# One-hop corner transfers, a later tile stage and one direct pair fewer in a spectral and gated-MLP kernel

## The chip, the cores and the metric

The kernel runs on one core of a Trainium2 chip. The metric is the device time in microseconds (us) of one execution.

## The reference

For x of 2048 tokens by 576 features (all float32), a two-dimensional Fourier filter and a gated MLP are mixed by a gate of each token:

```python
g = sigmoid((x * gate_w).sum(-1, keepdims=True))
X = jnp.fft.rfft2(x, axes=(-2, -1)) * (w_r + 1j * w_i)
a = jnp.fft.irfft2(X, s=(2048, 576), axes=(-2, -1))
h = jax.nn.gelu(x @ w_gate, approximate=True) * (x @ w_up)   # 576 -> 4608
b = h @ w_down                                               # 4608 -> 576
out = g * a + (1 - g) * b
```

## The kernel before

**The MLP, on TensorE.** Each float32 operand is kept as a high and a low part, and a product is three matmuls: high by high, high by low, low by high. The 4608 hidden features are 36 blocks of 128, taken two at a time ("a pair"), and the tokens are two halves of 1024; half by half that makes 36 pair turns, in the order of the string `PLAN` (line 35). A letter "c" is a direct pair (`conv`): eight chains of 14 matmuls of 512 columns, that is 112. An "s" is a pair by block products (`products`): the operands are cut into 2 by 2 blocks, and seven products of sums stand for eight; with two chains of seven matmuls each that is 98. Both kinds end in the same eight `down` turns (one for 128 tokens, 12 matmuls of 288 columns into PSUM tile `pdn`, two buffers), which ScalarE empties into `stg` (four buffers, L978); POOL adds them to the DRAM tiles `yd` by accumulating DMA (L965). `PLAN` is 2 direct pairs, 10 as block products, 10 direct, 14 as block products. The direct ones are needed where the operand sums of the block products have no room: `operands` puts those sums in tile `sx`, which lies in the same memory as `til`, the spectral tiles.

Weights are loaded by SP into `wq` (L834 direct, L1145 block products, L839 for `down`), split by ScalarE (`copy`, L218) and VectorE (L856, L1160, L1177).

**The filter, beside it.** `spectral` is a Python generator that emits the transforms a few instructions at a time. Row transforms (along the 576 features) run on VectorE and ScalarE in tile `rows`; column transforms (along the 2048 tokens) are a 4 by 4 tile stage (butterflies L96 to L104, twiddles L116 to L132) over the 16 blocks of `til`, and, in `columns`, a matrix product of length 128 of each block on TensorE (L283), the filter weights, and the product back. Then comes the inverse tile stage (`last_tiles`), half by half of the blocks, stores to the DRAM tile `bw` (`kept`, L733), and in the last stretch of block products `fetch` (L644), `fetched_rows` and `inverse_rows`, whose result is added to `yd`.

**How the order is made.** Each engine runs its instructions in the order in which they are emitted. `gap` is called after every product chain and every `down` turn: it runs what was put off to this gap, and lets the generator emit as long as its credit lasts. Credit is what the matmuls emitted since then take on PE; each VectorE instruction emitted is charged. A bare `yield None` ends the generator's turn in this gap. A direct pair has 24 gaps, a block-product pair 22. When the second stretch of "s" begins, `operands(1)` has to be done, and at the last pair the generator has to be empty; otherwise `gap` is called without matmuls.

**The column stage.** `columns` takes the 16 blocks in turn, six steps (gaps) each; `kb` is the block. A block's two halves, real and imaginary, lie so that the transform needs one quarter of each exchanged between partitions 0 to 63 and 64 to 127: the corners. `corner` does this in two hops over a small buffer `cns` (in `hx`), two transfers of 64 partitions out (L272, L273) and two back (L269, L270), all issued by SP, once ahead of the forward product and once behind the inverse one:

```python
if g == 0: v = product(0, kb, xh, xl); load_ww(kb + 1); corner(kb + 2, 0, False)
if g == 1: copy(xh2, two(Z[kb + 1])); corner(kb - 2, 2, True)
if g == 3: swap(); corner(kb + 2, 0, True); low(xl2, two(Z[kb + 1]), xh2)
if g == 4: w = product(1, kb - 1, yh, yl)      # copied back into Z[kb - 1]
if g == 5: filter_end(); corner(kb - 1, 2, False)
```

Beside this, `beside` emits the inverse butterfly of four blocks (`four`) five steps into the sixth block of each group, `while gone[0] < (4 * d + 5) * STEP + 5`.

## Time and profile before

| what | value |
|---|---|
| median of 3 runs | 1359.33 us (1356.89 to 1361.45) |
| profiled execution, its own time | 1353.73 us |
| its span, first to last instruction | 1352.0 us |
| granted TensorE clock, mean | 0.998 |
| DMA | 231.95 MB, mean 172 GB/s |
| direct pairs 12 to 21, with the column stage | about 425 to 847 us of the span |
| last stretch of block products | from about 847 us |

A page of the profile gives the busy time of each engine (PE is the matmuls, PEld the weight loads, DVE VectorE, ACT ScalarE, POOL GpSimd, SP the queue of the loads and stores), and the chain of work that ended last, which says what set the end. The views by window give the busy time in a stretch; the timeline shows in brackets how long an engine stood still ahead of an instruction and what released it. A matmul of 512 columns starts 0.23 us after the one before, though a row gives it 0.39.

### The profile page before, as it was taken

How to read it: one execution, taken by the hardware profiler on the slowest of the kernel's cores; microseconds unless marked ns; L12 is line 12 of the kernel's file. 1: busy time of each engine (PE TensorE's matmuls, PEld its weight loads, DVE VectorE, ACT ScalarE, POOL GpSimd, SP SyncE). 2: the span in 40 equal slices, each digit the busy share in tenths (PEclk: the TensorE clock that was granted, in tenths of full speed). 3: DMA queues.
4: the chain of work that ended last, by engine and by line, in shares of the span. 5: the costliest groups of instructions: out<-in, count | busy, mean ns of one | idle time of the engine just before them, and what ended most of it. 6: DMA issues, size and time to landing. Idle time of an engine off the chain costs nothing.

```text
span 1352.0 us, 20022 instructions
## 1 busy us (share of the span) xinstructions
PE 1335.8 (99%) x7353; PEld 1180.6 (87%) x7353; DVE 1112.5 (82%) x1566; ACT 839.3 (62%) x1446; POOL 263.3 (19%) x323
## 2 busy tenths in 40 slices
PE   9999999999999999999999999999999999999998
PEld 7888888888888888888888888888888888888887
DVE  7689999899898779777775885899996699998554
ACT  5766666666765445656654448666766766766762
POOL 0011212221212221222220111112222321122321
PEclk9999999999999999999999999999999999999999
DMA  8667776786667977999994776867668967766986
GB/s 313 200 144 152 149 140 138 180 196 127 120 115 148 226 169 171 208 234 257 253 226 136 218 207 139 214 127 133 129 133 152 219 130 134 134 130 130 166 189 176
DMA packets 112067, 231.95 MB, mean 172 GB/s; under 512 B 13024, under 2 KB 28896, under 8 KB 111584
## 3 DMA queue, kind: packets, MB, share of 16 engines
q0 software_dynamic: 44928, 90.98, 44.7%
q1 hardware_dynamic: 67040, 139.69, 31.4%
q8 instruction: 57, 0.93, 0.3%
q14 instruction: 42, 0.34, 0.1%
HBM read 124.09 MB, written 99.39 MB: 165 GB/s over the span
## 4 chain that ended last, share of the span: by engine, by line
PE 91%; ACT 2%; DVE 2%; DMA 2%; issue 1%; SPq 0%; DVEq 0%; ACTq 0%
PE pdn L952 32%; PE pgu L1195 6%; PE pgu L1197 6%; PE pgu L1196 6%; PE pone L1195 6%; PE pone L1197 5%; PE pone L1196 5%; PE pgu L877 4%; PE pgu L879 4%; PE pgu L878 4%; PE pgu L1198 3%; PE pone L1198 3%; PE pone L877 2%; PE pone L879 2%; PE pone L878 2%; PE pone L283 1%
## 5 line engine op out<-in xcount | busy, mean ns | idle before, releaser
L965 POOL DMA_DIRECT2D yd<-stg x264 | 229.0, 867 | 1011.4 <-ACT stg L978 789.5
L978 ACT ACTIVATE stg<-pdn,omg 128x576 f32<-128x576 f32 x276 | 204.2, 740 | 274.6 <-PE pdn L952 272.4
L952 PE MATMUL pdn<-dn,hb 128*128 128x288 f32 x2472 | 361.2, 295 | 0.3 <-DVE wq L1019 0.2
L952 PEld LDWEIGHTS pdn<-dn,hb 128*128 128x128 f32 x2472 | 347.7, 188 | 13.4 <-ACT stg L978 0.7
L218 ACT ACTIVATE gu<-wq 64x256 fp32r<-64x256 f32 (+4 forms) x365 | 236.1, 661 | 75.7 <-DVE gu L1160 54.3
L1160 DVE TENSOR_TENSOR gu<-wq,gu 128x768 fp32r<-128x768 f32 x168 | 159.7, 952 | 33.4 <-ACT gu L218 33.0
L952 PE MATMUL pdn<-dn,hx 128*128 128x288 f32 x960 | 148.3, 295 | 0.0
L952 PEld LDWEIGHTS pdn<-dn,hx 128*128 128x128 f32 x960 | 137.4, 188 | 4.1
L877 PE MATMUL pgu<-xhi,gu 128*128 128x512 f32 x276 | 108.7, 394 | 2.2 <-DVE gl L934 2.2
L878 PE MATMUL pgu<-xhi,gu 128*128 128x512 f32 x276 | 108.3, 392 | 0.0
L879 PE MATMUL pgu<-xlo,gu 128*128 128x512 f32 x276 | 108.2, 392 | 0.0
L1177 DVE TENSOR_TENSOR wq<-wq 128x768 f32<-128x768 f32 x96 | 91.2, 952 | 10.7 <-ACT gu L218 10.2
L218 ACT ACTIVATE hb<-gl 128x512 fp32r<-128x512 f32 x65 | 40.8, 628 | 50.0 <-DVE gl L934 47.8
L856 DVE TENSOR_TENSOR dn<-wq,dn 128x576 fp32r<-128x576 f32 x72 | 54.1, 752 | 10.8 <-ACT dn L218 10.7
L877 PEld LDWEIGHTS pgu<-xhi,gu 128*128 128x128 f32 x276 | 52.2, 189 | 11.6 <-DVE gl L934 3.0
L879 PEld LDWEIGHTS pgu<-xlo,gu 128*128 128x128 f32 x276 | 52.1, 189 | 11.6
L878 PEld LDWEIGHTS pgu<-xhi,gu 128*128 128x128 f32 x276 | 52.1, 189 | 8.5
L1195 PE MATMUL pgu<-xhi,gu 128*128 128x512 f32 x144 | 56.8, 394 | 2.7 <-ACT pgu L218 2.7
L1195 PE MATMUL pone<-xhi,gu 128*128 128x512 f32 x144 | 56.6, 393 | 0.1
L1195 PE MATMUL pgu<-sx,gu 128*128 128x512 f32 x144 | 56.5, 392 | 0.0
L1195 PE MATMUL pone<-sx,gu 128*128 128x512 f32 x144 | 56.4, 392 | 0.0
L1197 PE MATMUL pgu<-xlo,gu 128*128 128x512 f32 x144 | 56.2, 391 | 0.0
(246 smaller groups left out, 2829.7 us busy)
## 6 DMA issues: line engine op xcount, KB each, us to landing
yd<-stg POOLq DMA_DIRECT2D x264, 288.0 KB, 4.9
wq<-ws SPq DMA_DIRECT2D x96, 384.0 KB, 4.4
wq<-wd SPq DMA_DIRECT2D x72, 288.0 KB, 5.2
wq<-wgu SPq DMA_DIRECT2D x22, 640.0 KB, 6.3
colm<-col POOLq DMA_DIRECT2D x32, 256.0 KB, 6.3
misc<-wf SPq DMA_DIRECT2D x16, 290.0 KB, 6.0
hx<-til SPq DMA_DIRECT2D x64, 72.5 KB, 5.5
til<-hx SPq DMA_DIRECT2D x64, 72.5 KB, 4.4
```

The source lines that it names most:

```text
L218: act.activation(o, i, AF.Copy)
L877: pe.matmul(ps, w[:, 0, k, c], xhi[tb][:, k], start=k == 0, stop=False)
L878: pe.matmul(ps, w[:, 1, k, c], xhi[tb][:, k], start=False, stop=False)
L879: pe.matmul(ps, w[:, 0, k, c], xlo[tb][:, k], start=False, stop=False)
L952: pe.matmul(ps[half], h[:, l, c], d[:, k, half * HD:(half + 1) * HD], start=part == 0 and n == 0, stop=part == 1 and n == 2)
L965: pl.dma_start(yd[u], o, accum_op=ALU.add)
L978: put(u, lambda o: act.activation(o.rearrange("p (c k) -> p c k", c=2), v[:, :, 0:HD], AF.Copy, scale=omg[:, u:u + 1]), i == 0)
L1160: vec.tensor_tensor(o, x.rearrange("p (c k) -> p c k", c=3), f(w[:, 256:1024]).rearrange("p (c k) -> p c k", c=3), ALU.subtract)
L1177: at(lead, lambda: vec.tensor_tensor(o, u, v, ALU.subtract))
L1195: pe.matmul(ps, hi, xh[:, t], start=start and t == 0, stop=False, skip_group_check=True)
L1196: pe.matmul(ps, lo, xh[:, t], start=False, stop=False, skip_group_check=True)
L1197: pe.matmul(ps, hi, xl[:, t], start=False, stop=False, skip_group_check=True)
```

## The change

Three things change together:

- `PLAN` has 9 direct pairs in the middle instead of 10, and 15 pairs as block products at the end instead of 14.
- A corner exchange is one hop of four transfers of 64 partitions instead of two hops of two. Ahead of the forward product the whole block, exchanged, goes from `til` into one of two buffers `near` (in `hx`); behind the inverse product the result is first copied into one of two buffers `far` (in `xraw`), and goes from there, exchanged, into `til`. The inverse butterflies may start two steps earlier, and the loop is one block shorter.
- The inverse tile stage of half one (blocks e = 0 and 1 of each group) leaves the direct stretch. `keep` stores the four-block results to `bw` within the column stage, two stores of 290 KB each time; in the last stretch `late_tiles(0)` and `late_tiles(1)` load four blocks into `tmp` (1160 KB), do twiddles and butterfly there, and write `rows` directly. `last_tiles(1)`, `kept(1)` and `operands(1)` follow the columns as before.

```diff
-PLAN = "c" * 2 + "s" * 10 + "c" * 10 + "s" * 14
+PLAN = "c" * 2 + "s" * 10 + "c" * 9 + "s" * 15
...
+            near = [f(hx)[:, SW * i:SW * (i + 1)] for i in range(2)]
+            far = [flat[:, SW * i:SW * (i + 1)] for i in range(1, 3)]
-            def corner(kb, slot, back):
+            def corner(kb, back):
...
-                z, c = two(Z[kb]), cns[:, slot + kb % 2]
+                o, i = two(near[kb % 2]), two(Z[kb])
                 if back:
-                    nc.sync.dma_start(z[0:64, 1], c[0:64])
-                    nc.sync.dma_start(z[64:128, 0], c[64:128])
-                else:
-                    nc.sync.dma_start(c[0:64], z[64:128, 0])
-                    nc.sync.dma_start(c[64:128], z[0:64, 1])
+                    o, i = i, two(far[kb % 2])
+                for c in range(2):
+                    for al in range(2):
+                        nc.sync.dma_start(o[64 * c:64 * c + 64, al], i[64 * al:64 * al + 64, c])
...
-                    while gone[0] < (4 * d + 5) * STEP + 5:
+                    while gone[0] < (4 * d + 5) * STEP + 3:
                         yield None
                     yield from four(d, range(4), sp, 1)
+                    keep(d)
+                    yield None
...
-            for kb in range(18):
+            for kb in range(17):
...
-                            corner(kb + 2, 0, False)
+                            corner(kb + 2, False)
...
-                            copy(xh2, two(Z[kb + 1]))
-                        corner(kb - 2, 2, True)
+                            copy(xh, near[(kb + 1) % 2])
...
-                            corner(kb + 2, 0, True)
                         if kb + 1 < 16:
-                            low(xl2, two(Z[kb + 1]), xh2)
+                            low(xl, near[(kb + 1) % 2], xh)
...
-                                copy(two(Z[kb - 1])[:, al], w[al][:, :NK])
+                                copy(two(far[(kb - 1) % 2])[:, al], w[al][:, :NK])
...
-                            corner(kb - 1, 2, False)
+                            corner(kb - 1, True)
...
+        def keep(d):
+            for e in range(2):
+                c = slice(SW * (4 * e + d), SW * (4 * e + d + 1))
+                nc.sync.dma_start(bw[:, c], til[0][:, c])
+
+        def late_tiles(e):
+
+            nc.sync.dma_start(tmp[:, 0:4 * SW], bw[:, 4 * SW * e:4 * SW * (e + 1)])
+            for _ in range(5):
+                yield None
...
+            x = [tmp[:, SW * i:SW * (i + 1)] for i in range(4)]
+            *tmps, sp = (rows[:, i:i + SW] for i in (UNIT, UNIT + SW, 3 * UNIT, 3 * UNIT + SW))
...
+            if o:
+                yield from _twiddles(vec, act, lambda d, e: x[d], lambda d, e: x[d][:, re], lambda d, e: x[d][:, im],
+                                     [((k, e), o * k) for k in range(1, 4)], tmps, 1, 0.39)
+            yield from _butterfly(vec, lambda i: x[i], lambda i: x[i][:, re], lambda i: x[i][:, im],
+                                  range(4), sp, 1, (0.69, 0.39))
...
+                pl.memset(rows.rearrange("p (c g k) -> p c g k", c=2, g=4)[:, :, g, 2 * KF:], 0.0)
...
             yield from last_tiles(1)
-            yield from with_stores(last_tiles(0), kept(1))
-            yield from with_stores(operands(1), kept(0))
+            yield from with_stores(operands(1), kept(1))
             yield from until(3)
-            fetch(0, 0, places_of[0])
-            yield from fetched_rows(0)
+            yield from late_tiles(0)
+            yield from late_tiles(1)
+            fetch(1, 0, places_of[1])
             yield from inverse_rows(0)
-            yield from fetched_rows(1)
+            yield from fetched_rows()
             yield from inverse_rows(1)
```

Three places show how this moves instructions. The first is SP's queue in the middle of the column stage: `hx` and `til` are the corners, `wf` the filter's weights. Before, one block's turn:

```order
L261 DMA tmp<-wf 128x580 x2
L272 DMA hx<-til 64x290
L273 DMA hx<-til 64x290
L269 DMA til<-hx 64x290
L270 DMA til<-hx 64x290
L269 DMA til<-hx 64x290
L270 DMA til<-hx 64x290
L272 DMA hx<-til 64x290
L273 DMA hx<-til 64x290
```

Now, a turn at which a group of four blocks has been finished, and the next one:

```order
L260 DMA tmp<-wf 128x580 x2
L274 DMA hx<-til 64x290 x4
L640 DMA bw<-til 128x580 x2
L274 DMA til<-xraw 64x290 x4
L260 DMA misc<-wf 128x580 x2
L274 DMA hx<-til 64x290 x4
L860 DMA wq<-wgu 128x1280
L274 DMA til<-xraw 64x290 x4
```

A turn still has eight corner transfers, but none that needs another one of its block to have landed; the stores of `keep` stand between them.

The second is SP's queue where the direct pairs end and the last stretch begins (`ws` and `wd` are weights, `xhi`, `xlo`, `misc` and `tmp` the places for `bw`). Before:

```order
L733 DMA bw<-til 128x1160 x4
L839 DMA wq<-wd 128x576 x2
L733 DMA bw<-til 128x1160 x4
L1145 DMA wq<-ws 128x768 x4
L839 DMA wq<-wd 128x576 x2
L644 DMA xhi_64<-bw 128x2x290
L644 DMA xlo_66<-bw 128x2x290
L644 DMA misc<-bw 128x2x290 x2
L644 DMA tmp<-bw 128x2x290 x4
```

Now:

```order
L759 DMA bw<-til 128x1160 x4
L1171 DMA wq<-ws 128x768 x4
L865 DMA wq<-wd 128x576 x2
L644 DMA tmp<-bw 128x2320
L1171 DMA wq<-ws 128x768 x4
L865 DMA wq<-wd 128x576 x2
L644 DMA tmp<-bw 128x2320
L1171 DMA wq<-ws 128x768 x4
L865 DMA wq<-wd 128x576 x2
L675 DMA xhi_64<-bw 128x2x290
```

Four of the eight wide stores are gone, and two loads of four blocks stand a pair apart among the weights where eight loads stood together.

The third is VectorE at the end of pair 11, the last block-product pair ahead of the direct ones; the instruction on `gu` makes the low part of a direct pair's weights, the one on `xraw` and `pgu` is the last gelu product of pair 11. Before:

```order
L1233 TENSOR_TENSOR xraw<-xraw,pone 128x512
L856 TENSOR_TENSOR gu_71<-wq,gu_71 128x1280
L1219 TENSOR_TENSOR hx<-xraw,hx 128x512
L96 TENSOR_TENSOR rows<-rows 128x40x32
L1216 TENSOR_TENSOR xraw<-xraw 128x512
L101 TENSOR_TENSOR rows<-rows 128x20x32
L1290 TENSOR_TENSOR xraw<-xraw,pgu 128x512
L101 TENSOR_TENSOR rows<-rows 128x20x32 x3
```

Now:

```order
L1259 TENSOR_TENSOR xraw<-xraw,pone 128x512
L1245 TENSOR_TENSOR hx<-xraw,hx 128x512
L1242 TENSOR_TENSOR xraw<-xraw 128x512
L101 TENSOR_TENSOR rows<-rows 128x20x32
L1316 TENSOR_TENSOR xraw<-xraw,pgu 128x512
L882 TENSOR_TENSOR gu_72<-wq,gu_72 128x1280
L101 TENSOR_TENSOR rows<-rows 128x20x32 x2
```

With nine direct pairs the first one's weights go into buffer `gu_72` instead of `gu_71`, which comes free later, and their low part moves from ahead of that product to behind it.

More of the change, by code (lines that the diff above doesn't have):

```diff
@@ L653, in fetched_rows @@
             s2 = sgn[:, None, :].to_broadcast([P, 2, KF])
[L654 to L655 removed]
+            for b in range(2):
+                for i, x in enumerate(places_of[1]):
                     g, c = divmod(i, 2)
```

53 lines of the change are left out of this document (28 added, 25 removed).

## The prediction

> **What bounds the kernel now.** I read the page first (busy times and the chain), then the stages by window, then the PE waits inside the stages that lose time. The page's busy row and the chain:
>
> ```profile
> PE 1335.8 (99%) x7353; PEld 1180.6 (87%) x7353; DVE 1112.5 (82%) x1566; ACT 839.3 (62%) x1446; POOL 263.3 (19%) x323
> PE 91%; ACT 2%; DVE 2%; DMA 2%; issue 1%; SPq 0%; DVEq 0%; ACTq 0%
> ```
>
> TensorE is the bound: 91% of the chain. So time can go in two ways only: fewer matmuls, or fewer holes between them. The stages (columns: stretch, its length, busy us and instructions of PE, PEld, DVE, ACT, POOL, granted clock, DMA share, GB/s) show where the holes are:
>
> ```profile
> 535.00:720.00 185.00, 179.67 (x1007) 159.60 (x1006) 141.03 (x228) 109.73 (x187) 42.59 (x58) 0.99 0.92 228
> 720.00:860.00 140.00, 139.77 (x759) 122.59 (x758) 96.83 (x135) 79.74 (x130) 17.21 (x20) 1.00 0.69 182
> 860.00:1232.00 372.00, 372.00 (x2054) 329.34 (x2053) 338.91 (x447) 250.75 (x443) 80.41 (x94) 1.00 0.73 142
> 1232.00:1335.00 103.00, 103.00 (x577) 91.63 (x577) 57.62 (x78) 66.37 (x114) 26.88 (x31) 1.00 0.83 171
> ```
>
> The column stage (535 to 720) has 185 − 179.67 = 5.33 us without PE. The last stretch of block products has none. Inside the column stage:
>
> ```profile
> 580.00:600.00 20.00, 18.83 (x108) 16.56 (x107) 12.69 (x20) 10.72 (x18) 5.21 (x7) 1.00 0.96 247
> 620.00:640.00 20.00, 20.00 (x117) 17.98 (x116) 13.18 (x21) 13.18 (x23) 5.25 (x8) 1.00 1.02 255
> 680.00:700.00 20.00, 17.58 (x88) 15.29 (x88) 13.05 (x22) 8.75 (x16) 3.62 (x6) 0.91 1.01 278
> 700.00:720.00 20.00, 18.26 (x96) 15.49 (x96) 16.41 (x27) 11.72 (x21) 3.22 (x4) 1.00 0.68 145
> ```
>
> Three holes: 1.17, 2.42 and 1.74 us, which is the 5.33. The timeline names who waited (in brackets: idle time before the row, and its releaser):
>
> ```profile
> 596.47 1.56 DVE L96 TENSOR_TENSOR til<-til 128x580 f32<-128x580 f32 x2 [1.78 <-DMA til<-hx]
> 598.68 0.50 PE L877 MATMUL pgu<-xhi,gu 128*128 128x512 f32 x1 [1.17 <-DVE gl L934]
> 686.06 0.69 ACT L218 ACTIVATE colm<-til 128x580 fp32r<-128x580 f32 x1 [2.81 <-DMA til<-hx]
> 690.68 1.34 PE L283 MATMUL pone<-colm 128*128 128x290 f32 x4 [2.42 <-DVE colm L276]
> ```
>
> The first two both start at the second hop of a corner transfer. At 596 the inverse butterfly sits on VectorE waiting for its last block's corners, and the gelu product behind it comes late. At 686 ScalarE waits for a block's corners and everything of that block is late. The third hole has VectorE busy (16.41 of 20) and no transfer: it is crowding. The second hole also costs clock:
>
> ```profile
> 690.00:692.00 2.00, 1.32 (x5) 1.32 (x6) 1.90 (x3) 1.27 (x2) 0.00 (x0) 0.66 1.04 352
> 692.00:694.00 2.00, 2.00 (x7) 1.54 (x6) 0.73 (x2) 1.82 (x5) 0.57 (x1) 0.50 0.85 197
> ```
>
> At clocks of 0.66 and 0.50, 2 × 0.34 + 2 × 0.50 = 1.7 us of matmul time are lost besides the hole itself.
>
> **The change part by part.**
>
> *One direct pair becomes a block-product pair.* Rows of the chain at the same place of two neighbouring pairs (start, length):
>
> ```profile
> 740.18 3.18 PE pdn L952 x24
> 778.40 3.18 PE pdn L952 x24
> ...
> 945.13 3.18 PE pdn L952 x24
> 980.19 3.18 PE pdn L952 x24
> ```
>
> A direct pair takes 778.40 − 740.18 = 38.22 us, a block-product pair 980.19 − 945.13 = 35.06. The swap gives **−3.16 us**; no engine but PE has a say in it, as long as the others keep up.
>
> *Corners in one hop.* Number of transfers (128) and their size (72.5 KB) stay; the chain of two becomes one. For the two blocks of the holes the chain of work shows the hops (start of the issue, us to landing), and the timeline the issues on SP (second column: how long one took) and the copy ahead of them:
>
> ```profile
> 584.23 6.69 DMA hx<-til
> 591.51 4.77 DMA til<-hx
> ...
> 673.24 6.61 DMA hx<-til
> 680.43 5.54 DMA til<-hx
> ```
>
> ```profile
> 577.62 0.81 ACT L218 ACTIVATE til<-pone 128x290 f32<-128x290 f32 x2 [0.47 <-PE pone L283]
> ...
> 583.67 0.51 SPq L272 DMA_DIRECT2D hx<-til  x1
> ...
> 591.01 0.46 SPq L269 DMA_DIRECT2D til<-hx  x1
> ...
> 673.24 1.11 SPq L273 DMA_DIRECT2D hx<-til  x1
> ```
>
> Second hole: ScalarE wanted the block at 686.06 − 2.81 = 683.25, and it landed at 680.43 + 5.54 = 685.97. In one hop of four, two more issues follow the one of 673.24 (1.11 us). At 0.5 us each the last starts by 674.9 and lands 6.61 us on, at 681.5: 1.7 us before it is wanted. That hole goes: **−2.42, and −1.70 of clock**.
>
> First hole: the inverse products were copied out by 577.62 + 0.81 = 578.43. SP, held by other blocks' second hops, sent their corners at 583.67 and sent them back at 591.01; VectorE wanted them at 596.47 − 1.78 = 594.69. Sent once, even as late as before, they land two issues and 6.69 us after 584.23, at 591.9. The butterfly now starts two steps, that is two gaps, earlier; at 1.6 us a gap (below) VectorE wants them at 591.5. So the wait is 0.4 us if SP is as late as before and none if it isn't; with its second hops gone I take none: **−1.17**.
>
> What is late next there is the crowding: the butterfly's ten VectorE instructions now share their steps with the block filter's own. That costs between 0 and another 1.74, as at 700 to 720; I take half, **+0.87**, and leave the old 1.74 where it is.
>
> The 52 and 53 half-partition transfers issued in these 185 us land in 5.9 and 4.3 us (medians):
>
> ```profile
> til<-hx SPq DMA_DIRECT2D x53, 72.5 KB, 4.3
> hx<-til SPq DMA_DIRECT2D x52, 72.5 KB, 5.9
> ```
>
> One after the other they would take 53 × 4.3 + 52 × 5.9 = 535 us, so nearly three are in flight at once, and a hop of four costs only its two issues more than a hop of two. A rule of the Trainium skill speaks against this: "DMA: Bandwidth & Descriptors" (Rules for kernel authors) says that two transfers to disjoint partition halves serialize, and wants one 128-partition transfer instead. By that rule of the Trainium skill the four would land two behind two; rival 1 has the time for it. The trace does not agree so far as the landing times above go.
>
> On the clock term, the Trainium skill's "TensorE: Matmul & The Clock Gate" (What's actually happening) has the clock halve after some 3.4 us without work. By that page of the Trainium skill a 2.42 us hole would not have cost clock, and the gain would be 1.70 smaller. The two rows of 690 to 694 show that it did, so the term stays.
>
> *Half one's inverse tile stage moved.* It leaves the direct stretch (139.77 of 140 busy: nothing to win there) and runs in the last one, one block at a time. Wide instructions become pairs of narrow ones:
>
> ```profile
> 802.27 1.36 DVE L104 TENSOR_TENSOR til<-rows,til 128x1160 f32<-128x1160 f32 x1
> L104 DVE TENSOR_TENSOR til<-xraw,til 128x580 f32<-128x580 f32 x16 | 12.2, 760 | 0.3
> ```
>
> Two of 0.76 stand for one of 1.36. Twenty butterfly and ten twiddle instructions of at most 0.76 are at most 23 us of VectorE. Their cover: 372 − 338.91 = 33 us of idle VectorE, and the added pair, whose own need (57.62/103 × 35.06 = 19.6, from the last stretch's end, where no transform runs) leaves 15.4 more. So VectorE costs nothing; without that cover it would be the 23.
>
> Its loads tmp<-bw (1160 KB each) are new. The first is issued as soon as tmp is free, well ahead of its use. The second is issued behind the last read of the first, and ScalarE wants it six gaps later; a block-product pair has 22 gaps (14 chains, 8 token blocks), so a gap is 35.06/22 = 1.59 us, and six are 9.56. The nearest rows, a store of 1280 KB and (last row) the loads rows<-fw of 640 KB:
>
> ```profile
> fw<-rows SPq DMA_DIRECT2D x2, 1280.0 KB, 9.6
> DMA to landing us min/median/max: 7.2/9.6/13.4
> ```
>
> 9.6 and an issue of 0.5 make a wait of 0.5 us; by the last row it lies between none and 4.3. I take **+0.5**. Queued behind the waiting ScalarE are the evacuations of pdn, and PE waits for those once its two buffers are full. Behind the load on SP are weights with a pair's lead. What the stage leaves behind in the direct stretch stays: ScalarE's wait for the stores of half two, 6.49 us, which cost PE nothing there.
>
> ```profile
> 812.74 1.16 ACT L218 ACTIVATE sx<-tmp 128x512 fp32r<-128x512 f32 x2 [6.49 <-DMA bw<-til]
> ```
>
> *The rest at nothing.* The low part of the first direct weight now stands behind the gelu product of pair 11:
>
> ```profile
> 418.58 1.48 DVE L856 TENSOR_TENSOR gu<-wq,gu 128x1280 fp32r<-128x1280 f32 x1
> 423.32 0.68 DVE L1290 TENSOR_TENSOR xraw<-xraw,pgu 128x512 f32<-128x512 f32 x1
> 424.97 0.39 PE L878 MATMUL pone<-xhi,gu 128*128 128x512 f32 x1
> ```
>
> The 1.48 moves from ahead of L1290 to behind it: that can then start 1.48 earlier, and the low part ends at 424.0, before 424.97; if L1290 stays put, 425.5: at most +0.5. POOL's small memsets wait for VectorE with yd<-stg behind them (four buffers of stg). In POOL's order eight additions from `stg` follow the inverse's last one to yd, where twelve did; the last reads of yd come behind them all. The `keep` stores hold SP until VectorE has ended a butterfly, with corners behind them that have 1.7 us to spare. The longest hold of such a store was
>
> ```profile
> SPq L733 <- DVE til L104: 18.0, 2, 10.4
> ```
>
> 10.4 us, where SP had run ahead with nothing older queued. In the column stage other transfers always stand ahead of it; I take none, at most 10.4 − 1.7 = 8.7 once.
>
> *Sum.* −3.16 − 1.17 − 2.42 − 1.70 + 0.87 + 0.5 = **−7.08 us**. The profiled execution took 1353.73 us (span 1352.0), so 1346.65; the median of the runs is 5.60 above it, and the terms carry over: 1359.33 − 7.08 = **1352.2 us**.
>
> **The rivals.**
>
> 1. *The hop is no shorter.* If the four transfers land two behind two, 6.61 and 5.54 us add up again and both holes stay. For it: a DMA share near 1 in this stage. Against it: the 535 us above. This is what the Trainium skill's rule above would do. Time: 1359.33 − 3.16 + 0.87 + 0.5 = 1357.5. Chance 0.20.
> 2. *The late load stops ScalarE.* 13.4 + 0.5 − 9.56 = 4.3 us of wait and as much PE, in place of 0.5: 1356.0. Against it: the DMA share is 0.73 there. Chance 0.09.
> 3. *DMA becomes the bound of the column stage: slower.* Eight stores of 290 KB are added to it; at its 228 GB/s that is 10.4 us of all engines, where 0.92 of 185 us is taken. It decides if the engines are really full: then the weights (640 KB, four waits already) come late and PE takes it all.
>
> ```profile
> ACT gu L218 <- DMA wq<-wgu: 4.5, 4, 2.1
> ```
>
> With the holes staying too: 1359.33 − 3.16 + 10.4 + 0.87 + 0.5 = 1367.9. Against it: from 620 to 640 the share is 1.02 and PE loses nothing. Chance 0.07.
>
> **How the numbers follow.** Forecast 0.64, rivals 0.20, 0.09, 0.07. A measurement of this kernel tells 0.3%, or 4.1 us, from no change. The forecast (1351 with crowding and load at none, 1355 with the crowding at 1.74 and a load wait of 2.5) lies below 1359.33 − 4.1 = 1355.2; rivals 1 and 2 lie within 0.3%, with a little of them below: faster 0.66, same 0.27, slower 0.07. The range goes down to all holes gone and nothing new, 1359.33 − 3.16 − 5.33 − 1.70 = 1349.1, and 2 us of scatter, 1347; up to rival 1 with its 2 us, 1359.5.
>
> **What would show it.** Right: no PE hole from a til or hx transfer in the column stage and no clock below 1.00 there; 35.06 us for one pair more; PE full in the stretch of the late tiles. Wrong: a wait of ScalarE for tmp<-bw over 2 us with PE idle behind it, PE waits for VectorE in the column stage of over 4 us, or c weights waited for.

## The result, and the profile after

| what | before | after |
|---|---|---|
| median of the runs beside each other | 1358.11 us (1354.12 to 1361.45, 6 runs) | 1346.69 us (1346.24 to 1348.01, 6 runs) |
| profiled execution, its own time | 1353.73 us | 1348.01 us |
| its span | 1352.0 us | 1346.2 us |

The ratio is 0.9918, interval 0.9900 to 0.9936. The change makes the kernel faster, by more than forecast: 1346.69 lies 0.3 us under the low end of the range. Two things stand out before any line is read. The runs after lie within 1.8 us of each other, those before within 7.3. And from profile to profile the time fell by 5.72 us, less than the 7.08 forecast, while the median fell by 11.4 (12.64 from the 1359.33 that the forecast started from). The profiled execution after is the longest of its six.

The page of the kernel after, busy times and the shares of the chain:

```profile
PE 1331.9 (99%) x7339; PEld 1178.5 (88%) x7339; DVE 1122.2 (83%) x1589; ACT 847.7 (63%) x1464; POOL 263.7 (20%) x326
PE 90%; DVE 4%; ACT 3%; DMA 2%; issue 1%; SPq 1%; DVEq 0%; ACTq 0%
```

Fourteen matmuls fewer (7353 to 7339), TensorE still the bound. The stages by window, same columns as before:

```profile
535.00:720.00 185.00, 182.70 (x1042) 163.34 (x1041) 148.49 (x243) 116.85 (x199) 42.90 (x59) 1.00 0.99 245
720.00:820.00 100.00, 97.92 (x519) 85.77 (x518) 66.31 (x91) 56.35 (x94) 10.37 (x12) 0.98 0.65 175
820.00:1232.00 412.00, 412.00 (x2275) 364.83 (x2274) 374.00 (x502) 280.44 (x494) 88.86 (x106) 1.00 0.73 143
```

The column stage's idle time went from 5.33 to 2.30 us. The last stretch, now with the late tiles, is still full: 412.00 of 412. New is a loss of 2.08 us and some clock between them. The column stage closer, at the places of the old holes:

```profile
580.00:600.00 20.00, 20.00 (x116) 17.93 (x116) 15.73 (x27) 12.34 (x21) 5.22 (x7) 1.00 1.12 278
680.00:700.00 20.00, 18.58 (x100) 15.94 (x99) 17.34 (x30) 11.19 (x22) 3.17 (x5) 1.00 0.83 221
700.00:720.00 20.00, 19.12 (x108) 16.80 (x107) 14.87 (x24) 12.10 (x20) 2.27 (x3) 1.00 0.79 195
690.00:692.00 2.00, 2.00 (x11) 1.65 (x11) 1.96 (x5) 2.00 (x5) 0.00 (x0) 1.00 0.20 50
692.00:694.00 2.00, 2.00 (x18) 2.00 (x17) 1.97 (x5) 0.50 (x2) 0.00 (x0) 1.00 0.92 293
```

The first hole (1.17) is gone, the second is 1.42 instead of 2.42 and the third 0.88 instead of 1.74, and the clock between 690 and 694 is 1.00 where it was 0.66 and 0.50. The timeline names another releaser for what is left:

```profile
688.55 0.50 PE L903 MATMUL pgu<-xhi,gu 128*128 128x512 f32 x1 [1.42 <-DVE gl L960]
709.61 0.80 PE L284 MATMUL pone<-colm 128*128 128x290 f32 x4 [0.88 <-DVE colm L277]
```

Both wait for VectorE, none for a transfer: what is left there is crowding. The transfers themselves in this stretch (number, size, us to landing):

```profile
til<-xraw SPq DMA_DIRECT2D x60, 72.5 KB, 5.4
hx<-til SPq DMA_DIRECT2D x49, 72.5 KB, 6.7
```

They land a little later than before (4.3 and 5.9), but a block needs one hop of them where it needed two. The new loss lies behind SP's four stores of half two and ScalarE's first copy into `sx`, which needs them to have landed (the row's releaser reads "issue"; the last store landed at 769.30, by its semaphore, 0.2 us ahead of that copy):

```profile
757.47 3.82 SPq L759 DMA_DIRECT2D bw<-til  x4
...
769.52 0.63 ACT L217 ACTIVATE sx<-tmp 128x512 fp32r<-128x512 f32 x1 [10.53 <-issue]
...
775.57 1.81 PE L978 MATMUL pdn<-dn,hb 128*128 128x288 f32 x7 [1.86 <-ACT hb L217]
```

ScalarE stands still for 10.53 us there, where it stood for 6.49 before, and TensorE loses 1.86 us behind it and then clock:

```profile
774.00:776.00 2.00, 0.43 (x3) 0.43 (x4) 0.64 (x2) 1.98 (x4) 0.10 (x1) 1.00 1.03 137
776.00:778.00 2.00, 2.00 (x10) 1.84 (x9) 1.44 (x3) 1.95 (x4) 0.00 (x0) 0.58 0.61 106
778.00:780.00 2.00, 2.00 (x10) 1.98 (x9) 1.29 (x2) 1.94 (x5) 0.00 (x0) 0.57 0.00 0
```

The other five runs have spans of 1344.5 to 1345.0 against 1346.2; that they lack the clock share of this loss fits, but they were not profiled.

The sum from profile to profile, with the matmul starts of both traces (how much each one comes later than the usual step of its line): the column stage, 500 to 750 us, lost 10.04 us before and 4.60 after; 750 to 900 us lost 1.86 and 5.22; what follows the end of the last matmul shrank from 4.83 to 4.29. −3.16 − 5.44 + 3.36 − 0.54 = −5.78, which is the difference of the spans (5.8).

### The profile page after: what moved, and what is told of

Same layout as the page of the kernel before. It is cut to its first block, busy times and chain, and to the rows that moved or that the text cites. A ratio compares the mean times of both kernels' runs of the same rounds, so it can differ in the third digit from the quotient of the medians.

```text
span 1346.2 us, 20091 instructions
## 1 busy us (share of the span) xinstructions
PE 1331.9 (99%) x7339; PEld 1178.5 (88%) x7339; DVE 1122.2 (83%) x1589; ACT 847.7 (63%) x1464; POOL 263.7 (20%) x326
## 4 chain that ended last, share of the span: by engine, by line
PE 90%; DVE 4%; ACT 3%; DMA 2%; issue 1%; SPq 1%; DVEq 0%; ACTq 0%
PE pdn L978 31%; PE pgu L1221 6%; PE pone L1221 6%; PE pgu L1223 6%; PE pgu L1222 6%; PE pone L1223 6%; PE pone L1222 6%; PE pgu L905 4%; PE pgu L903 4%; PE pgu L904 4%; PE pgu L1224 3%; PE pone L1224 3%; PE pone L284 2%; PE pone L904 1%; PE pone L905 1%; PE pone L903 1%
## 5 line engine op out<-in xcount | busy, mean ns | idle before, releaser
L978 PE MATMUL pdn<-dn,hb 128*128 128x288 f32 x2424 | 355.4, 296 | 2.1 <-ACT hb L217 1.9
L978 PEld LDWEIGHTS pdn<-dn,hb 128*128 128x128 f32 x2424 | 342.7, 189 | 15.1 <-ACT hb L217 2.1
L217 ACT ACTIVATE gu<-wq 64x256 fp32r<-64x256 f32 (+4 forms) x377 | 241.6, 655 | 69.8 <-DVE gu L1186 48.7
L1186 DVE TENSOR_TENSOR gu<-wq,gu 128x768 fp32r<-128x768 f32 x175 | 166.8, 954 | 37.2 <-ACT gu L217 36.6
L978 PE MATMUL pdn<-dn,hx 128*128 128x288 f32 x1008 | 154.9, 295 | 0.0
L978 PEld LDWEIGHTS pdn<-dn,hx 128*128 128x128 f32 x1008 | 143.9, 188 | 4.1
L903 PE MATMUL pgu<-xhi,gu 128*128 128x512 f32 x256 | 100.2, 391 | 1.4 <-DVE gl L960 1.4
L1203 DVE TENSOR_TENSOR wq<-wq 128x768 f32<-128x768 f32 x100 | 95.1, 954 | 6.7 <-ACT gu L217 6.1
L905 PE MATMUL pgu<-xlo,gu 128*128 128x512 f32 x256 | 100.1, 391 | 0.0
L904 PE MATMUL pgu<-xhi,gu 128*128 128x512 f32 x256 | 100.0, 390 | 0.0
L1221 PE MATMUL pgu<-xhi,gu 128*128 128x512 f32 x152 | 59.8, 393 | 2.5 <-ACT pgu L217 2.5
L1221 PE MATMUL pgu<-sx,gu 128*128 128x512 f32 x152 | 59.6, 392 | 0.0
L1223 PE MATMUL pgu<-xlo,gu 128*128 128x512 f32 x152 | 59.4, 391 | 0.0
L1223 PE MATMUL pgu<-sx,gu 128*128 128x512 f32 x152 | 59.3, 390 | 0.0
L1222 PE MATMUL pgu<-xhi,gu 128*128 128x512 f32 x152 | 59.3, 390 | 0.0
L1222 PE MATMUL pgu<-sx,gu 128*128 128x512 f32 x152 | 59.2, 390 | 0.0
L1224 PE MATMUL pgu<-sx,gu 128*128 128x512 f32 x152 | 59.1, 389 | 0.0
```

The source lines that it names most:

```text
L217: act.activation(o, i, AF.Copy)
L903: pe.matmul(ps, w[:, 0, k, c], xhi[tb][:, k], start=k == 0, stop=False)
L904: pe.matmul(ps, w[:, 1, k, c], xhi[tb][:, k], start=False, stop=False)
L905: pe.matmul(ps, w[:, 0, k, c], xlo[tb][:, k], start=False, stop=False)
L978: pe.matmul(ps[half], h[:, l, c], d[:, k, half * HD:(half + 1) * HD], start=part == 0 and n == 0, stop=part == 1 and n == 2)
L1186: vec.tensor_tensor(o, x.rearrange("p (c k) -> p c k", c=3), f(w[:, 256:1024]).rearrange("p (c k) -> p c k", c=3), ALU.subtract)
```

## The experiments

Each was measured beside runs of the kernel before on the same chip; where a ratio is given, it is to those. Medians of two variants from different sessions are a looser comparison: the kernel before itself had session medians from 1355.8 to 1359.47 us. "Kernel after" and "kernel before" are the two of the study.

**The kernel before, again.** No edit.

> The kernel before, unchanged. Theory A (the gain beyond the forecast 7.08 us comes from corner waits, whose size changes from one execution to the next, and the one profiled execution had few of them): times spread over some 7 us again (1354 to 1361), with a lower mean clock in the longer ones, and this profile has other holes at til<-hx in the column stage than the 1.17 and 2.42 us of the first. Theory B (the rest of the change is worth more than its 3.16 us): the spread has nothing to do with the column stage; its holes are again 5.3 us in all.

1357.72 us (1352.9 to 1361.0, 12 runs), ratio 0.9999 (0.9982 to 1.0016). The spread is the kernel's own, and the 1359.33 that the forecast started from lay some 2 us above the median of all its 70 runs in the sessions with many (1357.47; by session 1358.11, 1357.26, 1355.8 and 1359.47). The profiled execution took 1355.63 us; in its column stage ScalarE waited up to 4.4 us for a corner where the first profile had 2.8, and VectorE's butterfly 0.8 where it had 1.8:

```profile
ACT colm L218 <- DMA til<-hx: 8.1, 4, 4.4
DVE til L96 <- DMA til<-hx: 0.8, 1, 0.8
```

That the waits change in size from one execution to the next is as Theory A has it. How much of the spread they make, one profile doesn't say.

**One hop, old plan.** The kernel before with the `columns` and `corner` of the kernel after, without `keep`; the earlier start of the inverse butterflies went with them, so this is the hop and the two steps together:

```diff
-                    while gone[0] < (4 * d + 5) * STEP + 5:
+                    while gone[0] < (4 * d + 5) * STEP + 3:
-                    nc.sync.dma_start(c[0:64], z[64:128, 0])
-                    nc.sync.dma_start(c[64:128], z[0:64, 1])
+                for c in range(2):
+                    for al in range(2):
+                        nc.sync.dma_start(o[64 * c:64 * c + 64, al], i[64 * al:64 * al + 64, c])
```

> The kernel before with the one-hop corners and the earlier inverse butterfly alone: ten direct pairs, both halves' tile stage in the direct stretch. Theory A: about 8 us faster than before (11.4 measured for the whole change less 3.16 for the pair), 1350, and its executions lie within 2 us of each other. Theory B: 2.72 + 1.70 = 4.4 us faster, 1353.7, with the spread of before.

1351.24 us (1350.84 to 1352.51, 6 runs), ratio 0.9963 (0.9949 to 0.9976), against 1357.26 in that session. So hop and start alone give 5 to 6 us where the forecast's terms for it made 4.42, and it takes the spread from 9 us to 1.7, as Theory A said (its 8 us did not come). The rest of the change is 1351.24 − 1346.69 = 4.55 us across two sessions, where the forecast had 3.16 − 0.5. The profiles place most of it: 3.16 of the swap, and the stretch behind the column stage, this run first and then the kernel after:

```profile
720.00:860.00 140.00, 137.18 (x733) 120.43 (x732) 91.64 (x125) 75.64 (x124) 17.33 (x20) 0.99 0.70 177
```

```profile
720.00:860.00 140.00, 137.92 (x731) 120.68 (x730) 96.89 (x139) 86.58 (x148) 17.65 (x22) 0.99 0.66 172
```

The kernel after loses 0.74 us less there, and no late load costs anything: 3.9, and the spans differ by 4.0 (1350.2 and 1346.2).

**Two hops in the kernel after.** The reverse: `columns` of the kernel before, with `keep` added.

```diff
-                    while gone[0] < (4 * d + 5) * STEP + 3:
+                    while gone[0] < (4 * d + 5) * STEP + 5:
-                for c in range(2):
-                    for al in range(2):
-                        nc.sync.dma_start(o[64 * c:64 * c + 64, al], i[64 * al:64 * al + 64, c])
+                    nc.sync.dma_start(c[0:64], z[64:128, 0])
+                    nc.sync.dma_start(c[64:128], z[0:64, 1])
```

> The changed kernel with the two-hop corners put back; three turns at the start of the last stretch have no matmuls then. Theory A: 3.16 us or a little less faster than before, about 1355 to 1356, spread over some 7 us as before. Theory B: 11.4 - 4.4 = 7 us faster, about 1351.

1365.88 us (1363.72 to 1368.55), ratio 1.0069 (1.0052 to 1.0086): slower than the kernel before, and neither theory's number. The column stage and the stretch behind it:

```profile
535.00:720.00 185.00, 176.95 (x982) 157.31 (x980) 138.20 (x223) 108.58 (x185) 42.57 (x59) 0.97 0.94 234
720.00:860.00 140.00, 131.20 (x678) 114.40 (x679) 91.87 (x135) 77.23 (x130) 13.47 (x16) 0.95 0.58 155
```

The corner holes are back (8.05 us idle), and 8.80 us are lost behind them: with the shorter plan the two-hop column stage ends too late for the operand sums, and, as the expectation has it, three gaps run without matmuls at the start of the last stretch. The new corner exchange, hop and start together, is thus what the other two parts stand on.

**The shorter plan in the kernel before.**

```diff
-PLAN = "c" * 2 + "s" * 10 + "c" * 10 + "s" * 14
+PLAN = "c" * 2 + "s" * 10 + "c" * 9 + "s" * 15
```

> The kernel before, with the new order of pairs alone (nine direct, fifteen as block products): two hops and the tile stage of half one where they were. The operand sums are then not done when the last stretch begins, and 17 gaps are run without matmuls. Theory A (the moved tile stage is what makes the pair's 3.16 us reachable): TensorE stands still for 17 to 27 us at about 810 us, so 1357.3 - 3.2 + 17 to 27, that is 1371 to 1381 us. Theory B (the parts add up one by one; the gaps without matmuls are filled with work that would have been done anyway and gives time back later): 1354 to 1358 us.

1377.87 us (1374.46 to 1381.9, 4 runs), ratio 1.0156 (1.0121 to 1.0192): Theory A. The window behind the column stage:

```profile
720.00:860.00 140.00, 117.67 (x611) 101.79 (x612) 95.27 (x136) 75.63 (x127) 11.81 (x14) 0.90 0.58 164
```

TensorE stands 22.33 us there. The 3.16 us of the swap are reachable only because other parts of the change empty the direct stretch.

**The stores ahead of the sums.** The kernel after, with half two's four stores issued together, five empty gaps behind them, and then the operand sums:

```diff
-            yield from with_stores(operands(1), kept(1))
+            for i in range(4):
+                c = slice(8 * SW + 2 * SW * (3 - i), 8 * SW + 2 * SW * (4 - i))
+                nc.sync.dma_start(bw[:, c], til[0][:, c])
+            for _ in range(5):
+                yield None
+            yield from operands(1)
```

> The changed kernel with the four stores of half two issued together right behind its tile stage and five turns of the generator left free before the operand sums begin. If the new hole at 774 us (1.86 us, and a clock of 0.91 over 20 us behind it) comes from ScalarE's 10.5 us wait for these stores, it goes: 2 to 3.7 us less in the profiled execution, 1 to 3 us in the median, about 1344.5. Rival: the wait only moves with the first copy into sx, and the time stays at 1346.7.

1345.89 us (1345.44 to 1346.12, 5 runs), ratio 0.9921 (0.9906 to 0.9936); none of its runs reaches one of the kernel after, but the gain is 0.8 us across two sessions where 1 to 3 were expected. The loss at 774 us is gone. Two smaller ones came at 807 and 810 us (0.79 and 0.89 us by the matmul starts), since the sums now end two gaps ahead of the last stretch.

**The corner issued later.** The kernel after, its forward transfers written three steps later:

```diff
                     if g == 0:
                         if on:
                             v = product(0, kb, xh, xl)
                             load_ww(kb + 1)
-                            corner(kb + 2, False)
...
                     elif g == 3:
                         if on:
                             swap()
+                            corner(kb + 2, False)
```

> The kernel after, with one line moved: the four transfers ahead of the forward product are issued three steps (4.8 us) later, at g == 3 instead of g == 0. The corner is then wanted four steps, about 6.4 us, behind its issue, which is what the second hop had in the kernel before; in the kernel after it is seven steps, about 11 us. Theory A (what the one hop bought is this slack, since transfers land in 5 to 7 us with a spread of some us): the waits come back, holes on TensorE behind the copy of a block in the column stage, some of them over 2 us with a lower clock behind them; 1350 to 1354 us, and runs that lie further apart than the 1.8 us of the kernel after. Theory B (what it bought is that no transfer waits for another one; how early it is issued matters little): 1346.7 us, within 0.5.

1347.51 us (1346.43 to 1348.58, 6 runs), ratio 0.9930 (0.9903 to 0.9956). The time fits Theory B, but the run doesn't test what it was meant to. The same transfers by source line, kernel after first, then this one (ns min/median/max of an issue, first and last start in us):

```profile
L274 SPq DMA_DIRECT2D hx<-til x64: 461/587/1151, 503.1 to 680.2; - x64
```

```profile
L274 SPq DMA_DIRECT2D hx<-til x64: 461/592/1658, 503.7 to 682.6; - x64
```

The line moved by three steps, some 4.8 us; 50 of the 64 transfers moved by less than 1 us, since SP was held in front of them by the block before (its `til<-xraw` waits for the copy into `xraw`: nine waits, 28.0 us in all in this column stage). How much slack the hop needs stays open.

**The butterflies later, in the kernel after.**

```diff
-                    while gone[0] < (4 * d + 5) * STEP + 3:
+                    while gone[0] < (4 * d + 5) * STEP + 5:
```

> The kernel after, with the inverse butterflies starting two steps later, as they did before (5 instead of 3). The prediction's crowding: the earlier start lays ten VectorE instructions on the block filter's own and costs 0.87 us; then the later start wins it back, 1345.8 us, and the small holes at 687 and 708 us of the span shrink. Rival: the earlier start costs nothing and the small holes are the block filter's own; then 1346.7 us, within 0.5. The operand sums end five gaps later by this, two gaps ahead of the last stretch instead of seven; if that is too little, a hole comes at about 806 us and adds 1 to 2 us.

1354.72 us (1353.65 to 1355.42, 12 runs), ratio 0.9983 (0.9968 to 0.9999). Both expectations fell: two steps are worth 8.0 us by these medians, 5.8 from profile to profile. The copies of the blocks ahead of their forward product (the last time is that of the last block), kernel after first, then this one:

```profile
L217 ACT ACTIVATE colm<-hx x5: 677/680/685, 642.0 to 691.5; 128x580 fp32r<-128x580 f32 x5
```

```profile
L217 ACT ACTIVATE colm<-hx x5: 678/687/691, 643.8 to 698.8; 128x580 fp32r<-128x580 f32 x5
```

The last block comes 7.3 us later. A likely reason, which no run tests by itself: the generator hands out VectorE time by credit, and butterflies that start late use the credit of the steps in which the next blocks should go on. By the matmul starts only 1.9 of the 5.8 us are lost within the column stage (6.52 against 4.60); 3.1 are lost from 750 to 900 us (8.35 against 5.22), most of it in one hole behind ScalarE's wait for the stores:

```profile
781.37 1.15 ACT L217 ACTIVATE sx<-tmp 128x512 fp32r<-128x512 f32 x2 [10.70 <-DMA bw<-til]
...
785.76 2.66 PE L978 MATMUL pdn<-dn,hb 128*128 128x288 f32 x12 [3.83 <-ACT stg L1004]
```

**The late load with less cover.** The kernel after, one empty gap instead of five behind a load of `late_tiles`:

```diff
-            for _ in range(5):
+            for _ in range(1):
```

> The kernel after, with one empty gap instead of five between a load of the late tiles and its use. The second load is issued at 847.3 us and lands 5.3 us later; two gaps behind the issue, 3.2 us, ScalarE or VectorE wants it and waits about 2.4 us. Theory A (the prediction's pricing: a wait there holds the evacuations of pdn and TensorE pays it in full): 1349.1 us, and a hole of 2.4 us near 852 us. Theory B (two buffers of pdn and the work queued ahead cover a wait of some 8 us, as 6.49 us of waiting cost nothing in the kernel before and 10.53 us cost 1.9 in the kernel after): 1346.7 us, within 0.5, and no hole there.

1348.1 us (1346.31 to 1351.98, 7 runs), ratio 0.9935 (0.9912 to 0.9958). The median says little, since its runs scatter by 5.7 us; the place says more:

```profile
820.00:1232.00 412.00, 412.00 (x2277) 364.88 (x2276) 377.06 (x505) 278.96 (x493) 88.19 (x105) 1.00 0.74 144
```

In the longest of its runs, which is the one profiled, TensorE is full throughout the stretch. But the wait of 2.4 us from which both theories start did not come: ScalarE was emptying `pdn` until 852.17, the load landed at 852.27, and ScalarE read it at 852.29. So the load needs less cover than it had, and neither theory of what a wait would cost is tested. What that run lost against the kernel after, it lost ahead of the edit, here from 40 to 100 us (56.29 us busy, where the kernel after has 58.38):

```profile
40.00:100.00 60.00, 56.29 (x284) 48.45 (x283) 43.49 (x65) 42.36 (x74) 4.47 (x5) 0.97 0.57 156
```

**One hop with the old start.** The kernel of "One hop, old plan", with 5 instead of 3:

```diff
-                    while gone[0] < (4 * d + 5) * STEP + 3:
+                    while gone[0] < (4 * d + 5) * STEP + 5:
```

> The kernel before with one-hop corners, and with the inverse butterflies started at the step at which it started them (5); the run with one hop alone had them two steps earlier (3) and took 1351.2 us. Theory H (the shorter hop is what gained 6 us): 1351.2 us, within 1, and runs within 2 us of each other. Theory S (the two steps are what gained it, since the run of the kernel after with the later start took 1354.7 us against 1346.7): 1355 to 1357 us, that is, nearly all of the gain gone, with the holes of the column stage behind VectorE and not behind a transfer.

1356.68 us (1355.19 to 1357.63, 12 runs), ratio 0.9982 (0.9971 to 0.9992), beside 1359.47 (1354.91 to 1362.31, 17 runs) of the kernel before. Theory S. Nothing in the column stage waits for a corner transfer any more, yet there are these 20 us of it, by window:

```profile
700.00:720.00 20.00, 16.71 (x92) 14.37 (x92) 16.09 (x28) 10.26 (x19) 2.34 (x3) 1.00 0.70 139
```

The wait in them, by the timeline:

```profile
706.18 0.80 PE L284 MATMUL pone<-colm 128*128 128x290 f32 x4 [2.25 <-DVE colm L277]
```

And a wait behind the column stage, ScalarE's for the stores and TensorE's for the evacuation queued behind it:

```profile
804.99 1.15 ACT L217 ACTIVATE sx<-tmp 128x512 fp32r<-128x512 f32 x2 [7.37 <-DMA bw<-til]
806.82 1.60 PE L946 MATMUL pdn<-dn,hb 128*128 128x288 f32 x7 [4.12 <-ACT stg L972]
```

The holes moved behind VectorE (3.29 us in these 20 us, where there were 1.74) and behind the stores. The hop alone leaves the shortest times where they were (1355.19 against 1354.91) and cuts the long ones. Yet in the column stage it gained: by the matmul starts 6.6 us are lost there instead of 10.0. What it gained was lost again behind it, 7.2 us from 750 to 900 instead of 1.9.

**Two hops with the early start.** The kernel before with 3 instead of 5:

```diff
-                    while gone[0] < (4 * d + 5) * STEP + 5:
+                    while gone[0] < (4 * d + 5) * STEP + 3:
```

> The kernel before, two hops and the old order of pairs, with the inverse butterflies started two steps earlier (3 instead of 5). The second hop of a group's last block is then issued two steps, 3.2 us, ahead of the butterfly that needs it, and lands 4.3 us or more behind its issue. Theory H: VectorE waits for it in each of the three butterflies inside the loop, TensorE behind it; 1356 to 1361 us, no gain. Theory S: the earlier start is worth having without the shorter hop; 1351 to 1353 us.

1366.83 us (1364.22 to 1369.57, 6 runs), ratio 1.0061 (1.0040 to 1.0081): Theory H's mechanism, with a higher price. The waits of its column stage (total, times, longest):

```profile
DVE til L96 <- DMA til<-hx: 14.6, 3, 7.5
```

The longest of them, by the timeline:

```profile
599.68 1.56 DVE L96 TENSOR_TENSOR til<-til 128x580 f32<-128x580 f32 x2 [7.48 <-DMA til<-hx]
...
604.55 0.80 PE L877 MATMUL pgu<-xhi,gu 128*128 128x512 f32 x1 [6.51 <-DVE gl L934]
```

VectorE waits 14.6 us for second hops in three butterflies, and TensorE behind it. Hop and start in one table (us, ratios to the kernel before):

| | butterflies at step 5 | at step 3 |
|---|---|---|
| two hops | the kernel before | 1366.83, 1.0061 (1.0040 to 1.0081) |
| one hop | 1356.68, 0.9982 (0.9971 to 0.9992) | 1351.24, 0.9963 (0.9949 to 0.9976) |

Neither is the gain by itself. What each does, and where, by the matmul starts of the profiles (us lost):

| | two hops, step 5 | two hops, step 3 | one hop, step 5 | one hop, step 3 |
|---|---|---|---|---|
| column stage, 500 to 750 us | 10.0 (9.4 to 13.8 in six executions) | 20.9 | 6.6 | 4.7 |
| behind it, 750 to 900 us | 1.9 | 5.6 | 7.2 | 5.6 |

The hop makes the early start possible. Within the column stage the hop gains 3.5 us without it, against the first profile of the kernel before, and more against most of the others; the early start gains 1.9 more. In the time of the whole kernel the hop alone gains little because the stretch behind, with ScalarE's wait for the stores, gets dearer. What the hop with the late start would gain without that wait was not run.

**Earlier still.** The kernel after with 1 instead of 3:

```diff
-                    while gone[0] < (4 * d + 5) * STEP + 3:
+                    while gone[0] < (4 * d + 5) * STEP + 1:
```

> The kernel after, with the inverse butterflies started two steps earlier still (1 instead of 3). The transfers of a group's last block are then issued two steps, 3.2 us, ahead of it and land 5.1 us behind their issue, with three more issues of 0.57 us ahead of the last. Landing theory (the start can go no further forward than the one hop lets it): VectorE waits about 3.5 us in each of three butterflies; holes of up to 3 us with a lower clock behind them, 1349 to 1355 us. Dose theory (the earlier the better): 1346.7 us or less, no holes from til<-xraw.

1348.98 us (1347.39 to 1351.06, 6 runs), ratio 0.9928 (0.9908 to 0.9948): about 2 us above the kernel after, across two sessions, and the intervals of the ratios overlap. The landing theory's waits didn't come, only one:

```profile
DVE tmp L221 <- DMA til<-xraw: 1.2, 1, 1.2
```

By the matmul starts its column stage lost 5.5 us against 4.6, spread over several places; no hole is larger by more than 0.6 us, so the cause is not shown. The dose theory has no support: three is not bettered by one.

**The stores ahead, three gaps.** As "The stores ahead of the sums", with three empty gaps:

```diff
-            for _ in range(5):
+            for _ in range(3):
```

> The kernel after with the stores of half two issued together ahead of the operand sums, and three empty gaps behind them where the earlier run of this kind had five and took 1345.9 us. ScalarE's wait for the stores is then some 5.7 us (10.53 less three gaps of 1.59), below the 6.49 that cost TensorE nothing in the kernel before: no hole at 774 us. The sums end four gaps ahead of the last stretch instead of two, so the two holes of 0.8 and 0.9 us at 806 to 808 us shrink: 1344.6 to 1345.9 us. If the wait below 6.5 us does cost, 1346.5 us.

1344.36 us (1343.86 to 1345.05, 5 runs), ratio 0.9895 (0.9876 to 0.9914). This is the fastest kernel of the study, 2.3 us below the kernel after, with no common run, though the two were measured in different sessions and the intervals of their ratios overlap. In the profiles 750 to 900 us lost 1.4 us against 5.2. ScalarE's wait is below the 6.49 us of the kernel before, and TensorE has no hole there:

```profile
768.96 1.15 ACT L217 ACTIVATE sx<-tmp 128x512 fp32r<-128x512 f32 x2 [5.07 <-DMA bw<-til]
```

```profile
720.00:860.00 140.00, 139.78 (x752) 122.50 (x751) 100.28 (x145) 89.96 (x153) 18.56 (x23) 1.00 0.68 181
```

**Four more executions of the kernel before.** No edit; where do its longer executions lose their time?

> The kernel before, unchanged, for one more profiled execution (the first of four). Two theories of why its median lies some 4 to 6 us above the execution that was profiled, while the kernel after stays within 1.8 us. Corner theory: a slower execution has longer holes behind corner transfers (near 597 and 687 us) and more matmuls at a lower clock behind them; an execution of 1358 us or more then shows at least 4 us more of such holes and slow matmuls than the 1353.73 us one, and equal holes elsewhere. Elsewhere theory: the difference lies outside the column stage (the start, the transitions, the last stretch), and the two corner holes are the same within 1 us.

> The kernel before, unchanged, the second of four more profiled executions, with the expectations of the first: by the corner theory the time above 1353 us is found within the column stage behind corner transfers, by the elsewhere theory outside it.

> The kernel before, unchanged, the third of four more profiled executions, with the expectations of the first: by the corner theory the time above 1353 us is found within the column stage behind corner transfers, by the elsewhere theory outside it.

> The kernel before, unchanged, the fourth of four more profiled executions, with the expectations of the first: by the corner theory the time above 1353 us is found within the column stage behind corner transfers, by the elsewhere theory outside it.

Times in that order: 1356.55, 1358.08, 1355.43 and 1357.64 us. The column stage of each, in the same order:

```profile
535.00:720.00 185.00, 179.66 (x1002) 159.48 (x1001) 141.95 (x231) 109.68 (x188) 43.10 (x59) 0.98 0.94 230
```

```profile
535.00:720.00 185.00, 177.45 (x996) 157.68 (x996) 140.64 (x228) 109.26 (x187) 42.62 (x58) 0.99 0.93 229
```

```profile
535.00:720.00 185.00, 179.82 (x1011) 160.17 (x1010) 141.51 (x230) 109.76 (x187) 42.59 (x58) 0.99 0.93 230
```

```profile
535.00:720.00 185.00, 176.96 (x987) 157.23 (x986) 138.67 (x224) 108.70 (x185) 42.62 (x58) 0.98 0.93 227
```

The butterfly of the first hole waited 1.7 us for `til<-hx` in the first of them, not at all in the third, and in the second and fourth:

```profile
598.53 1.56 DVE L96 TENSOR_TENSOR til<-til 128x580 f32<-128x580 f32 x2 [3.02 <-DMA til<-hx]
```

```profile
599.15 1.56 DVE L96 TENSOR_TENSOR til<-til 128x580 f32<-128x580 f32 x2 [4.40 <-DMA til<-hx]
```

By the matmul starts the column stage lost 10.8, 12.1, 9.4 and 13.8 us against 10.04 in the 1353.73 us execution. So in the fourth 3.7 of the 3.9 us more are there, in the second 2.0 of 4.4, in the first 0.7 of 2.8 (1.9 lie in the first 100 us), in the third none of 1.7. The corner theory's condition, 4 us in an execution of 1358 us, isn't met, and the elsewhere theory's isn't either: the wait at the first hole alone varies from none to 4.40 us. The column stage makes nearly all of the excess in one of the two longest and about half in the other, and what lies elsewhere is not explained. With the first profile and that of "The kernel before, again" (10.5) these are six executions of the kernel before: its column stage lost 9.4 to 13.8 us, 11.1 in the mean. With one hop and the early start it lost 3.9 to 4.7 in each of six (the kernel after, one hop with the old plan, both runs with the stores ahead, the corner issued later, the late load with less cover).

## Why the prediction was right or wrong

- **The swap, −3.16: right.** Fourteen matmuls fewer, and a pair in the last stretch takes 904.75 to 939.81, 35.06 us, as before:

```profile
904.75 3.18 PE pdn L978 x24
939.81 3.18 PE pdn L978 x24
```

- **First and second hole, −1.17 and −2.42: right about the waits, too dear in size.** No corner transfer is waited for in the column stage, in the kernel after or with one hop alone. But 1.42 us of the second hole stayed, behind VectorE. With the clock's −1.70 these terms made −5.29; the hop with the old start took 3.5 us out of the column stage of that execution.
- **The clock, −1.70: right** in the profiled executions.
- **Crowding, +0.87: wrong in sign, and the mis-sized part of the mechanism.** "the butterfly's ten VectorE instructions now share their steps with the block filter's own" took the earlier start for a cost. It took 1.9 us out of the column stage (6.6 to 4.7 in the old plan, 6.5 to 4.6 in the kernel after) and 1.7 and 3.1 out of the stretch behind it. In whole times the hop with the late start gives 0.18% (0.08 to 0.29), hop and early start together 0.37% (0.24 to 0.51). I costed the two steps by the instructions of one step instead of asking when the next block can go on. That the column stage as a whole came near its forecast (−5.44 for −4.42) is luck in part: the hop was put too dear by 1.8 us, the early start wrong by 2.8 the other way.
- **The late load, +0.5: no cost.** It landed 5.3 us behind its issue instead of 9.6, TensorE is full in the stretch, and with less cover the load still landed just as it was wanted.

```profile
tmp<-bw SPq DMA_DIRECT2D x2, 1160.0 KB, 5.3
```

- **"ScalarE's wait for the stores of half two, 6.49 us, which cost PE nothing there" stays: wrong.** The wait grew to 10.53 us and cost 1.86 us and some clock: the last store landed 9.32 us behind its issue instead of 6.79, and ScalarE stood at its copy 1.5 us behind the first issue instead of 2.6. One hop with the old plan had a wait of 10.50 there, so it did not come from the moved tile stage; why the stores landed later is not shown. With the stores ahead and three gaps the hole is gone, and the time 2.3 us lower, in another session. The length of such a wait is no price: 7.37 us cost 4.12 in the run of one hop with the old start, 10.53 cost 1.86.
- **"The terms carry over": the step that failed.** The sum was made against an execution of 1353.73 us and moved onto a median of 1359.33 unchanged, as if the 5.60 between them were a constant that the change leaves alone. It was not. The 1353.73 is the shortest of six profiled executions of the kernel before, whose mean is 1356.2, and the 1348.01 after is the longest of its six. So the 12.64 us are 5.72 from profile to profile, 2.45 because the first profile was a short one, 3.15 from the mean of the six to 1359.33 (some 2 of them because the first median was high), and 1.32 because the profile after was a long one. Part of what the longer executions lose is corner waits, some us larger than in the first profile, and those go with the hop: the column stage lost 9.4 to 13.8 us with two hops and 3.9 to 4.7 with one and the early start, and the hop with the old start has runs within 2.4 us where those of the kernel before beside it lie within 7.4. At the mean, 11.1, the column stage had 6.5 us to give, where the forecast had 4.42. That all of the offset was corner waits is not shown: in three of the four further executions half or more of the excess lies elsewhere.
- **The rest at nothing: right.** The change from block products to direct pairs and the `keep` stores left no hole: 100 to 535 us lost as much as before, and no transfer is waited for in the column stage. The 0.54 us gained behind the last matmul were in no term.
- **Rival 1** (the hop no shorter) fell. The Trainium skill's "DMA: Bandwidth & Descriptors" (Rules for kernel authors) has transfers to disjoint partition halves serialize. Here none was waited for. In the 32 hops of the kernel after, the four transfers landed within 0.5 to 4.5 us of each other, all of them 3.8 to 10.5 us behind the issue of the first; the two hops of the prediction's two blocks took 12.1 and 12.7. (The counts in flight, nearly three in the prediction and 3.5 here by the landing times above, don't decide it, since the time from issue to landing holds any queueing too.) But the time that the rival gave, 1357.5, is nearly what one hop with the old start took, by another mechanism. **Rival 2** fell with the late load. **Rival 3** fell as well: the DMA share rose to 0.99 and TensorE lost less.

## What to carry to other kernels

A profile is one execution: where a kernel's runs scatter by 9 us and the trace shows waits for chained transfers, ask how large these waits are in the longer executions before carrying terms to the median, since a change that removes the chain can remove much of the scatter too. After a latency is removed, see whether its consumer can be moved up, and look at the stretch behind: here the hop paid 3.5 us in its own stage and most of it was lost behind it. Price a move of work by what can go on because of it, and not only by the instructions that it lays on another step. A wait that costs nothing now can grow, and cost, when the work around it moves.

## What was not expected of the hardware

The clock fell behind rather short holes. Behind the 1.86 us hole of the kernel after it was 0.58 and 0.57 for 4 us (rows above), so the hole cost about as much again in clock. In the run of one hop with the old plan it fell in a hole of 2.59 us, too:

```profile
800.00:802.00 2.00, 0.59 (x2) 0.59 (x3) 1.93 (x4) 2.00 (x5) 0.35 (x1) 0.78 0.00 0
802.00:804.00 2.00, 2.00 (x11) 2.00 (x10) 1.75 (x3) 2.00 (x5) 0.68 (x2) 0.50 0.54 41
```

The some 3.4 us without work of the Trainium skill's "TensorE: Matmul & The Clock Gate" (What's actually happening) are not what these traces show. The traces' record of the clock has it at one half for 3.41 us each time: in the kernel before from 690.63, in the kernel after from 776.31, in this run from 801.13 (and for two and three times as long in "Two hops with the early start"). Matmuls of 288 columns start 0.24 us apart there instead of 0.13, so each such stretch costs up to 1.7 us. The length of the hole alone doesn't decide: one of 2.25 us (one hop with the old start, at 706.18) left the clock at 1.00, one of 1.67 ("Earlier still", at 776.67) did not.

The loads of 1160 KB landed in 5.3 us, sooner than the stores of 1280 KB (9.6) from which they were estimated.
